# Two casts a head turned into transfers between SBUF rows in a fused attention and expert kernel

## The chip, the cores and the metric

The kernel runs on one core of a Trainium2 chip. The metric is the device time of one launch in microseconds (us). A core has five engines with queues of their own: TensorE (PE: matmuls, and transposes as matmuls with the identity), VectorE (DVE), ScalarE (ACT), GpSimd (POOL) and SyncE (SP), which here does nothing but issue DMA transfers. An engine takes its instructions in the order in which they were written; one that waits holds all behind it. Operands lie in SBUF (128 rows, called partitions), matmul results in PSUM.

## The reference

Three stages follow one another. Attention: 2 batches of 8 heads, 768 positions, 64 dimensions, where a query sees only keys of its own cluster. Then a layer of 8 experts of which each token uses one, and then a dense layer with softplus. The change lies in the first stage, whose core is

```python
mask = q_assign[:, :, :, None] == k_assign[:, :, None, :]
scores = scale * np.matmul(q, k.transpose(0, 1, 3, 2))
scores = np.where(mask, scores, -1000000000.0)
scores = scores - np.max(scores, axis=-1, keepdims=True)
attn = np.exp(scores)
attn = attn / (np.sum(attn, axis=-1, keepdims=True) + 1e-09)
return np.matmul(attn, v).astype(np.float32)
```

`q_assign` and `k_assign` are the indices of the nearest of 16 centroids.

## The kernel before

**Precision.** TensorE is fed with fp32r, a rounded form of fp32. To keep the accuracy of fp32, the kernel splits q and k into a rounded high part and the rest. A head has four operand tiles of 768 columns. Of the 128 rows of kA, 64 hold the high part of k and the other 64 the same high part again; of qA, 64 rows hold the high part of q / 8 and 64 its rest. A matmul of the two so gives (q high + q rest) times k high (L304). qB holds the high part of q in rows 0 to 63, kB the rest of k, and a second matmul adds their product (L319). Rows 64 to 79 of qB and kB hold the clusters of queries and keys as one-hot rows with large factors: where they differ, the score goes far down. So the mask is part of the second matmul. These 16 rows are called the cluster rows here.

**The loop.** The 16 heads have 6 query tiles each, which gives 96 blocks g = 6 h + t (L1092). Block g does, in this order: the products of attention weights and v of the head before (`av_step`), the scores of block g + 2 and their row maximum on VectorE (`S_mm`, L309, nm at L321), the six transposes of the weights of block g and the copies from PSUM to SBUF (`P_T`, L335), then jobs that a table puts into this block, the exponential of block g + 2 on ScalarE (`S_exp`, L330), the table `after`, and last a part of the preparation of a later head. Nothing reorders this: program order is queue order on each engine. Score tiles and transposes have two PSUM buffers each.

**Preparation.** Head h (2 to 15) is prepared in four parts, at the ends of blocks 6 (h - 2) + 3 to 6 (h - 2) + 6 (`prep_part`, L268): both halves of kA, kB, then qA and qB. Its first scores are written into block 6 h - 2. `put_mask` (L289) then issues four transfers of 16 x 384 words on SyncE's queue, which put the cluster rows of the head into qB and kB; for heads 3 to 15 this follows part 3.

**What else is in the queues.** Heads come in pairs p. `load_raw` (L168) loads q and k of a pair into one of two buffers; it is written into block 12 p - 25 and waits for the last reader of the buffer, qA of head 2 p - 3 on VectorE (L285). Sixteen further jobs convert a weight matrix from 64-bit words: `cv_load` (L435) brings 1 MB (words), `cv_bits` (L443) works on it in the four blocks from g0 = 11 + 19 j / 4 on, first on ScalarE (cvd, L451) and then on VectorE, and `cv_store` (L467) writes 512 KB back (w_rows). In the blocks g0 + 1 to g0 + 3 the set `busy` puts both PSUM copies of the transposes on ScalarE; in the others the first is on VectorE. `sims_mm` and `sims_T` assign the clusters of a later pair, `fin_x` (L379) transposes the outputs of an earlier head (L385).

Of the kernel before, what the change touches and what calls it, by code (L numbers as in the profile page):

```python
# [8 lines left out]
F32 = mybir.dt.float32  # L9
# [4 lines left out]
AF = mybir.ActivationFunctionType  # L14
# [18 lines left out]
def body(ctx, tc, qT, kT, vP, cen, mod, wg, bias, w1, w2, win, wout, out):  # L33
# [5 lines left out]
    NT = S // 128  # L39
# [7 lines left out]
    pe, dve, act, pool, sp = nc.tensor, nc.vector, nc.scalar, nc.gpsimd, nc.sync  # L47
# [102 lines left out]
    busy = set()  # L150
# [4 lines left out]
    def drain():  # L155
        while pend:
            for _ in pend.pop(0):
                pass

    def run(f, *a):  # L160

        drain()
        x = f(*a)
        if hasattr(x, "__next__"):
            next(x, None)
            pend.append(x)
# [101 lines left out]
    def prep_part(h, i):  # L268

        p, o = h // 2, 64 * (h % 2)  # L270
        if i == 0:
            spl[h] = tuple(p_sp.tile([128, S], F32R, tag=n, name=n) for n in ("qA", "kA", "qB", "kB"))
        qA, kA, qB, kB = spl[h]
        q_s, k_s = (r[o:o + 64] for r in raw[p])
        hi, lo = slice(o, o + 64), slice(64 - o, 128 - o)
        if i == 0:
            act.copy(kA[hi], k_s)
        elif i == 1:
            act.copy(kA[lo], k_s)
            dve.tensor_tensor(out=kB[0:64], in0=k_s, in1=kA[hi].bitcast(F32), op=ALU.subtract)  # L280
        elif i == 2:
            act.activation(out=qA[hi], in_=q_s, func=AF.Copy, scale=0.125)
        else:
            act.activation(out=qB[0:64], in_=q_s, func=AF.Copy, scale=0.125)
            dve.scalar_tensor_tensor(  # L285
                out=qA[lo], in0=q_s, scalar=0.125, in1=qA[hi].bitcast(F32), op0=ALU.mult, op1=ALU.subtract
            )

    def put_mask(h):  # L289
        p, i = h // 2, h % 2  # L290
        qA, kA, qB, kB = spl[h]
        for j, x in enumerate((qB, kB)):
            for a in range(2):
                o = 64 * j + 32 * a + 16 * i
                sp.dma_start(
                    out=x[64:80, a * HS:(a + 1) * HS].bitcast(F32), in_=mks[p][o:o + 16].bitcast(F32)
                )
# [11 lines left out]
    def S_mm(g):  # L309
        if g >= NH * NT:  # L310
            return
        if g not in S_t:
            S_part(g)
        h, t = divmod(g, NT)
        qA, kA, qB, kB = spl[h]
        ps = S_t[g]
        ts = slice(t * 128, t * 128 + 128)
        for i in range(2):
            pe.matmul(ps[:, i, :HS], qB[:80, ts], kB[:80, i * HS:(i + 1) * HS], start=False, stop=True)  # L319
        nm_t[g] = p_m.tile([128, 1], F32, tag="nm", name="nm", bufs=4)  # L320
        dve.tensor_reduce(out=nm_t[g], in_=ps[:, :, :HS], axis=AX.XY, op=ALU.max, negate=True)  # L321

    def S_exp(g):
        if g >= NH * NT:
            return
        h, t = divmod(g, NT)
        if t == 0:
            sums[h] = p_m.tile([128, NT], F32, tag="sums", name="sums", bufs=3)
        P_t[g] = p_P.tile([128, 2, HS], F32, tag="P", name="P")
        act.activation(  # L330
            out=P_t[g], in_=S_t.pop(g)[:, :, :HS], func=AF.Exp, bias=nm_t.pop(g), scale=1.0,
            accum_out=sums[h][:, t:t + 1],
        )

    def P_T(g):  # L335
        h, t = divmod(g, NT)
        if t == 0:
            PT[h] = p_PT.tile([128, NT, S], F32, tag="PT", name="PT")
        P = P_t.pop(g)
        for i in range(2):  # L340
            ps = ps_T.tile([128, 3, 128], F32, tag="t", name="Tp")
            for j in range(3):
                pe.transpose(ps[:, j, :], P[:, i, j * 128:(j + 1) * 128], ident)  # L343
            dst = PT[h][:, 3 * i:3 * i + 3, t * 128:(t + 1) * 128]
            if i == 0 and g not in busy:
                dve.tensor_copy(dst, ps)
            else:
                act.copy(dst, ps)  # L348
# [20 lines left out]
    def av_step(g):  # L369

        h, kt = divmod(g - NT - 1, NT)
        if kt == NT - 1:
            return
        AV(h, kt)
        if kt == NT - 2:
            AV(h, NT - 1)
            fin_av(h)
# [566 lines left out]
    with tc.manual_schedule():  # L944
# [147 lines left out]
        for g in range(NH * NT):  # L1092
            h, t = divmod(g, NT)
            if g > NT:
                av_step(g)
            S_mm(g + 2)
            P_T(g)
            for f, a in jobs.get(g, ()):
                if inspect.isgeneratorfunction(f):
                    run(f, *a)  # L1100
                else:
                    f(*a)
            S_exp(g + 2)
            drain()
            for f, a in after.get(g, ()):
                f(*a)
            h2, i2 = divmod(g - 3, NT)
            h2 += 2
            if 2 <= h2 < NH and i2 < 4:
                prep_part(h2, i2)  # L1110
                if i2 == 3 and h2 > 2:
                    put_mask(h2)
            if g == 8:
                put_mask(2)
# [299 lines left out]
        for n in range(2, end):  # L1414
            kind, i, layer, s = seq[n]
# [149 lines left out]
        for c, y in enumerate((ys[NM - 1][1], ps_A.tile([128, 512], F32, tag="a", name="o"))):  # L1565
            cs = slice(c * 256, c * 256 + 256)
            for kt in range(16):
                gh, gl = gs[NM - 1, kt // 4]
                hi, lo = wts["out", kt // 2]
# [51 lines left out]
```

## Time and profile before

| | |
|---|---|
| median of 3 runs (lowest, highest) | 767.64 us (766.39, 768.34) |
| the profiled execution: its time, its span | 767.36 us, 765.6 us |
| TensorE (PE) busy | 708.8 us, 93% of the span |
| VectorE (DVE) busy | 450.0 us, 59% |
| ScalarE (ACT) busy | 416.1 us, 54% |
| GpSimd (POOL) busy | 128.5 us, 17% |
| mean granted clock of TensorE | 0.975 |

The span runs from the first to the last instruction. Shares of it are means over stages that differ: in the attention part, the first 300 us, VectorE and ScalarE are busy to eight or nine tenths, later to two or three. A row of a timeline gives start and duration of an instruction, or of several alike that follow one another (x2), and in brackets how long the engine had stood idle before it and what ended that. The granted clock is that of TensorE as a share of 2.4 GHz.

### The profile page before, as it was taken

How to read it: one execution, taken by the hardware profiler on the slowest of the kernel's cores; microseconds unless marked ns; L12 is line 12 of the kernel's file. 1: busy time of each engine (PE TensorE's matmuls, PEld its weight loads, DVE VectorE, ACT ScalarE, POOL GpSimd, SP SyncE). 2: the span in 40 equal slices, each digit the busy share in tenths (PEclk: the TensorE clock that was granted, in tenths of full speed). 3: DMA queues.
4: the chain of work that ended last, by engine and by line, in shares of the span. 5: the costliest groups of instructions: out<-in, count | busy, mean ns of one | idle time of the engine just before them, and what ended most of it. 6: DMA issues, size and time to landing. Idle time of an engine off the chain costs nothing. (4 is left out here: it accounts for less than half of the span.)

```text
span 765.6 us, 11692 instructions
## 1 busy us (share of the span) xinstructions
PE 708.8 (93%) x4498; PEld 564.4 (74%) x4498; DVE 450.0 (59%) x668; ACT 416.1 (54%) x663; POOL 128.5 (17%) x144
## 2 busy tenths in 40 slices
PE   4997997899798999986999999998999999999998
PEld 2764654556455555874879888997998898999887
DVE  5895987789789975863446563677143233233220
ACT  3886987798779976343446562663323323323310
POOL 4200000000310103635452522252000000000000
PEclk9898999999989999996999999999999999999999
DMA  4314454544553625979967985500010000000000
GB/s 133 105 56 174 145 198 151 171 145 160 183 131 119 199 98 167 236 110 368 355 228 277 345 301 195 179 15 20 10 42 15 28 15 15 15 1 28 1 28 27
DMA packets 38683, 99.28 MB, mean 130 GB/s; under 512 B 8255, under 2 KB 15615, under 8 KB 36577
## 3 DMA queue, kind: packets, MB, share of 16 engines
q1 hardware_dynamic: 35888, 91.42, 36.3%
q0 software_dynamic: 2592, 6.69, 2.4%
q8 instruction: 36, 0.59, 0.3%
q10 hardware_dynamic: 144, 0.39, 0.2%
q14 instruction: 23, 0.18, 0.1%
HBM read 79.13 MB, written 18.28 MB: 127 GB/s over the span
## 5 line engine op out<-in xcount | busy, mean ns | idle before, releaser
L1500 DVE SCALAR_TENSOR_TENSOR sp<-g,sp 128x1024 f32<-128x1024 f32 x24 | 29.4, 1224 | 148.8 <-ACT sp L1499 148.8
L321 DVE TENSOR_REDUCE nm<-S 128x1 f32<-128x768 f32 x96 | 90.9, 948 | 34.3 <-PE S L319 34.0
L1489 PE MATMUL g<-xh,wh 128*128 128x256 f32 x384 | 108.7, 283 | 0.0
L1489 PE MATMUL g<-xh,wl 128*128 128x256 f32 x384 | 107.9, 281 | 0.0
L1489 PE MATMUL g<-xl,wh 128*128 128x256 f32 x384 | 107.9, 281 | 0.0
L1497 ACT ACTIVATE sp<-g 128x1024 f32<-128x1024 f32 x24 | 24.6, 1027 | 136.6 <-PE g L1489 126.7
L330 ACT ACTIVATE P<-S,nm 128x768 f32<-128x768 f32 x96 | 86.9, 905 | 18.9 <-DVE nm L321 16.2
L343 PE MATMUL Tp<-ident,P 128*128 128x128 f32 x576 | 85.6, 284 | 10.7 <-ACT PT L348 7.5
L343 PEld LDWEIGHTS Tp<-ident,P 128*128 128x128 f32 x576 | 68.7, 144 | 24.5 <-ACT PT L348 14.2
L355 PE MATMUL av<-PT,v 128*64 128x384 f32 x384 | 80.7, 517 | 0.0
L741 POOL TENSOR_TENSOR wl<-raw,wh 128x1024 fp32r<-128x1024 f32 x22 | 54.1, 2469 | 139.2 <-ACT wh L740 132.2
L741 DVE TENSOR_TENSOR wl<-raw,wh 128x1024 fp32r<-128x1024 f32 x50 | 65.1, 1343 | 14.5 <-ACT wh L740 14.5
L1489 PEld LDWEIGHTS g<-xl,wh 128*128 128x128 f32 x384 | 73.0, 190 | 0.5
L740 ACT CAST wh<-raw 128x1024 fp32r<-128x1024 f32 x69 | 68.9, 1050 | 8.0 <-DMA raw<-in_w 5.4
L1489 PEld LDWEIGHTS g<-xh,wh 128*128 128x128 f32 x384 | 72.8, 190 | 0.5
L348 ACT COPY PT<-Tp 128x384 f32<-128x384 f32 x144 | 64.0, 477 | 16.8 <-PE Tp L343 16.0
L1489 PEld LDWEIGHTS g<-xh,wl 128*128 128x128 f32 x384 | 73.0, 190 | 0.0
L1524 PE MATMUL o<-wh,gT 128*128 128x512 f32 x216 | 69.7, 394 | 0.0
L319 PE MATMUL S<-kB,qB 80*128 80x384 f32 x192 | 51.8, 353 | 18.0 <-DMA kB<-mk 16.1
L843 PE MATMUL y<-wh,hT 128*128 128x512 f32 x192 | 64.7, 408 | 0.0
L304 PEld LDWEIGHTS S<-kA,qA 128*128 128x128 f32 x192 | 29.7, 194 | 47.1 <-ACT PT L348 16.2
L304 PE MATMUL S<-kA,qA 128*128 128x384 f32 x192 | 60.2, 396 | 1.2 <-ACT P L330 0.9
(284 smaller groups left out, 1396.9 us busy)
## 6 DMA issues: line engine op xcount, KB each, us to landing
raw<-in_w SPq DMA_DIRECT2D x56, 512.0 KB, 7.6
words<-in_win SPq DMA_DIRECT2D x8, 1024.0 KB, 7.4
w_rows<-cvt SPq DMA_DIRECT2D x16, 512.0 KB, 3.0
words<-in_wout SPq DMA_DIRECT2D x8, 1024.0 KB, 5.7
whole<-in_w SPq DMA_DIRECT2D x16, 512.0 KB, 6.2
raw<-w_rows SPq DMA_DIRECT2D x16, 512.0 KB, 4.6
rawq<-in_qT SPq DMA_DIRECT2D x8, 384.0 KB, 3.4
v<-in_vP SPq DMA_DIRECT2D x8, 384.0 KB, 3.4
```

The source lines that it names most:

```text
L304: pe.matmul(ps[:, i, :HS], qA[:, t * 128:t * 128 + 128], kA[:, i * HS:(i + 1) * HS], start=True, stop=False)
L319: pe.matmul(ps[:, i, :HS], qB[:80, ts], kB[:80, i * HS:(i + 1) * HS], start=False, stop=True)
L321: dve.tensor_reduce(out=nm_t[g], in_=ps[:, :, :HS], axis=AX.XY, op=ALU.max, negate=True)
L330: act.activation(out=P_t[g], in_=S_t.pop(g)[:, :, :HS], func=AF.Exp, bias=nm_t.pop(g), scale=1.0, accum_out=sums[h][:, t:t + 1],)
L343: pe.transpose(ps[:, j, :], P[:, i, j * 128:(j + 1) * 128], ident)
L348: act.copy(dst, ps)
L355: pe.matmul(av_t[h][64 * a:64 * a + 64, :], vt[p][:, kt, 64 * i:64 * i + 64], PT[h][:, kt, a * HS:(a + 1) * HS], start=(kt == 0), stop=(kt ...
L740: cp(self.hi, self.raw)
L741: eng.tensor_tensor(out=self.lo, in0=self.raw, in1=self.hi.bitcast(F32), op=ALU.subtract)
L843: pe.matmul(u["y"][j], x, y, start=(kt == 0 and i == 0), stop=(kt == 7 and i == 2))
L1489: pe.matmul(o, a, b[:, kt, :], start=(n == 0 and f % 2 == 0), stop=(n == 11), skip_group_check=True)
L1524: pe.matmul(ys[u][j], x[:, a:a + 128], y, start=(kt == 0 and i == 0), stop=(kt == 15 and i == 2))
```

## The change

Per head the second casts are gone: the second half of kA (L279) and qB (L284) are no longer written by ScalarE but copied by a DMA from the rows that the first casts have written. The scaled cast of q moves from part 2 to part 1, the subtraction for kB on VectorE from part 1 to part 2. The cluster rows of heads 3 to 15 are issued after part 0 and no longer after part 3. In blocks with t = 0 and 1 that are not in `busy` the first PSUM copy goes to ScalarE too; the table gives 15 such blocks.

```diff
         if i == 0:
             act.copy(kA[hi], k_s)
+            sp.dma_start(out=kA[lo].bitcast(F32), in_=kA[hi].bitcast(F32))
         elif i == 1:
-            act.copy(kA[lo], k_s)
+            act.activation(out=qA[hi], in_=q_s, func=AF.Copy, scale=0.125)
+            sp.dma_start(out=qB[0:64].bitcast(F32), in_=qA[hi].bitcast(F32))
+        elif i == 2:
             dve.tensor_tensor(out=kB[0:64], in0=k_s, in1=kA[hi].bitcast(F32), op=ALU.subtract)
-        elif i == 2:
-            act.activation(out=qA[hi], in_=q_s, func=AF.Copy, scale=0.125)
         else:
-            act.activation(out=qB[0:64], in_=q_s, func=AF.Copy, scale=0.125)
             dve.scalar_tensor_tensor(
                 out=qA[lo], in0=q_s, scalar=0.125, in1=qA[hi].bitcast(F32), op0=ALU.mult, op1=ALU.subtract
             )
...
             dst = PT[h][:, 3 * i:3 * i + 3, t * 128:(t + 1) * 128]
-            if i == 0 and g not in busy:
+            if i == 0 and g not in busy and (g - 6) % NT not in (0, 1):
                 dve.tensor_copy(dst, ps)
...
                 prep_part(h2, i2)
-                if i2 == 3 and h2 > 2:
+                if i2 == 0 and h2 > 2:
                     put_mask(h2)
```

SyncE's queue before, from the loads of pair 3 on (blocks 11 to 16); qB<-mk and kB<-mk are the cluster rows, here of head 3, and the two words are those of the conversions j = 1 and 2:

```order
L173 DMA rawq<-in_qT 128x768
L174 DMA rawk<-in_kT 128x768
L438 DMA words<-in_win 128x2048
L295 DMA qB<-mk 16x384 x2
L295 DMA kB<-mk 16x384 x2
L469 DMA w_rows<-cvt 128x1024
L438 DMA words<-in_win 128x2048
```

The same place now, from the transfers of head 3 (block 9) on; the second kA<-kA and the cluster rows behind it are those of head 4:

```order
L278 DMA kA<-kA 64x768
L295 DMA qB<-mk 16x384 x2
L295 DMA kB<-mk 16x384 x2
L281 DMA qB<-qA 64x768
L173 DMA rawq<-in_qT 128x768
L174 DMA rawk<-in_kT 128x768
L438 DMA words<-in_win 128x2048
L469 DMA w_rows<-cvt 128x1024
L278 DMA kA<-kA 64x768
L295 DMA qB<-mk 16x384 x2
L295 DMA kB<-mk 16x384 x2
L438 DMA words<-in_win 128x2048
```

The cluster rows of head 3 moved from behind the loads and the first words to ahead of them, and the second words moved behind the transfer and the cluster rows of head 4.

ScalarE before, from the start of the conversion j = 1 (end of block 15) to block 17; PT<-Tp are the PSUM copies of the transposes, kA and qA those of head 4:

```order
L451 ACTIVATE cvd<-words 128x1024
L277 CAST kA<-rawk 64x768
L348 COPY PT<-Tp 128x3x128 x2
L330 ACTIVATE P,sums<-S,nm 128x768
L191 COPY sim<-misc 128x384
L279 CAST kA<-rawk 64x768
L362 COPY xTu<-av 128x384
L348 COPY PT<-Tp 128x3x128 x2
L330 ACTIVATE P,sums<-S,nm 128x768
L216 COPY simT<-misc 128x384
L282 ACTIVATE qA<-rawq 64x768
```

The same place now:

```order
L451 ACTIVATE cvd<-words 128x1024
L277 CAST kA<-rawk 64x768
L348 COPY PT<-Tp 128x3x128 x2
L330 ACTIVATE P,sums<-S,nm 128x768
L191 COPY sim<-misc 128x384
L280 ACTIVATE qA<-rawq 64x768
L362 COPY xTu<-av 128x384
L348 COPY PT<-Tp 128x3x128 x2
L330 ACTIVATE P,sums<-S,nm 128x768
L216 COPY simT<-misc 128x384
```

The cast of q took the place of the second cast of k in block 16, and nothing stands in its old place in block 17.

## Rows read from the trace of the kernel before

**Rows 1.** Waits of PE, 20 to 300 us: total us, times, longest us.

```profile
PE S L319 <- DMA kB<-mk: 16.1, 5, 5.1
PE Tp L343 <- ACT PT L348: 7.5, 12, 1.3
```

**Rows 2.** Timeline of PE: start us, us, engine, line, instruction, count [idle before].

```profile
63.09 0.98 PE L319 MATMUL S<-kB,qB 80*128 80x384 f32 x2 [4.35 <-DMA kB<-mk]
...
72.12 0.55 PE L385 MATMUL misc<-ident,xTu 128*128 128x128 f32 x3 [0.20 <-ACT simT L216]
...
97.64 0.58 PE L319 MATMUL S<-kB,qB 80*128 80x384 f32 x2 [1.09 <-DMA kB<-mk]
...
104.52 0.55 PE L385 MATMUL misc<-ident,xTu 128*128 128x128 f32 x3 [0.16 <-ACT simT L216]
...
136.06 0.98 PE L319 MATMUL S<-kB,qB 80*128 80x384 f32 x2 [5.11 <-DMA kB<-mk]
...
144.50 0.55 PE L385 MATMUL misc<-ident,xTu 128*128 128x128 f32 x3 [0.20 <-ACT simT L216]
...
207.95 1.01 PE L319 MATMUL S<-kB,qB 80*128 80x384 f32 x2 [4.25 <-DMA kB<-mk]
...
217.90 0.55 PE L385 MATMUL misc<-ident,xTu 128*128 128x128 f32 x3 [0.20 <-ACT simT L216]
```

**Rows 3.** Timeline of SyncE's DMA queue, 53 to 59 us.

```profile
53.40 0.34 SPq L173 DMA_DIRECT2D rawq<-in_qT  x1
...
54.25 0.43 SPq L438 DMA_DIRECT2D words<-in_win  x1
54.78 1.25 SPq L295 DMA_DIRECT2D qB<-mk  x2
...
58.85 0.43 SPq L438 DMA_DIRECT2D words<-in_win  x1
```

**Rows 4.** Timeline of ScalarE around the three long waits.

```profile
62.50 1.12 ACT L451 ACTIVATE cvd<-words 128x1024 f32<-128x1024 f32 x1 [3.33 <-DMA words<-in_win]
63.53 0.82 ACT L277 CAST kA<-rawk 64x768 fp32r<-64x768 f32 x1
...
69.95 0.86 ACT L348 COPY PT<-Tp 128x384 f32<-128x384 f32 x2 [0.74 <-PE Tp L343]
70.69 0.92 ACT L330 ACTIVATE P<-S,nm 128x768 f32<-128x768 f32 x1
...
71.58 0.49 ACT L216 COPY simT<-misc 128x384 f32<-128x384 f32 x1
71.94 0.85 ACT L282 ACTIVATE qA<-rawq 64x768 fp32r<-64x768 f32 x1
72.68 0.84 ACT L348 COPY PT<-Tp 128x384 f32<-128x384 f32 x2
...
79.15 1.14 ACT L451 ACTIVATE cvd<-words 128x1024 f32<-128x1024 f32 x1
...
135.41 1.12 ACT L451 ACTIVATE cvd<-words 128x1024 f32<-128x1024 f32 x1 [4.37 <-DMA words<-in_win]
...
207.37 1.12 ACT L451 ACTIVATE cvd<-words 128x1024 f32<-128x1024 f32 x1 [3.75 <-DMA words<-in_wout]
```

**Rows 5.** Busy time of each engine, granted clock (PEclk), DMA share, GB/s.

```profile
66.00:67.00 1.00, 1.00 (x10) 0.28 (x4) 1.00 (x2) 0.90 (x3) 0.00 (x0) 0.50 0.04 16
...
68.00:69.00 1.00, 1.00 (x8) 0.40 (x5) 0.00 (x0) 0.47 (x2) 0.00 (x0) 1.00 0.00 0
```

**Rows 6.** Groups by line and shape, whole span: busy us, mean ns.

```profile
L348 ACT COPY PT<-Tp 128x384 f32<-128x384 f32 x144 | 64.0, 477 | 16.8 <-PE Tp L343 16.0
...
L280 DVE TENSOR_TENSOR kB<-rawk,kA 64x768 fp32r<-64x768 f32 x14 | 13.3, 949 | 0.1
```

**Rows 7.** DMA issues at 126.5 and 101.8 us: count, KB, us to landing.

```profile
words<-in_win SPq DMA_DIRECT2D x1, 1024.0 KB, 8.9
...
words<-in_win SPq DMA_DIRECT2D x1, 1024.0 KB, 5.9
```

## The prediction, made before the changed kernel was run

> **What bounds the kernel now.** I read the page's slices first: TensorE is busy nearly everywhere, and most of its idle slices lie in the first 300 us, the attention part. The waits of TensorE between 20 and 300 us then say what it stood still for [rows 1]. One line leads: the matmuls on the cluster rows waited 16.1 us in 5 waits for the transfers that put those rows into kB. Waits for ScalarE's PSUM copies add 7.5 us in 12.
>
> The timeline of TensorE shows where the 5 are: at the first score tile of heads 3, 5, 7, 9 and 11. Four of them are in [rows 2]; at heads 3, 7 and 11 they are long (4.35, 5.11 and 4.25, together 13.7), at heads 5 and 9 short (1.09, and what is left of 16.1, 1.3). Each of these matmuls starts a sequence that ends with the transposes of L385. Undisturbed it takes 104.52 - 97.64 = 6.88 us. After the long waits it takes 72.12 - 63.09 = 9.03, 8.44 and 9.95, that is 2.15, 1.56 and 3.07 more, 6.8 in all. The clock explains most of this: from 66 to 67 us the granted clock is 0.50 (1.2 GHz) while TensorE is busy throughout, and 1.00 (2.4 GHz) again from 68 us [rows 5]; it stood still before the clock fell. So the waits and their aftermath cost 16.1 + 6.8 = 22.9 us.
>
> Why the rows came late is read from SyncE's queue [rows 3]. It issued the loads of the next pair at 53.40, a weight load of 1 MB at 54.25, and the cluster rows of head 3 only at 54.78, behind both.
>
> ScalarE's timeline [rows 4] shows what a quick reading misses. At the same three places ScalarE itself stood for 3.33, 4.37 and 3.75 us, until that 1 MB load (words) had landed, and resumed at 62.50, 135.41 and 207.37: 0.6 us before TensorE each time. Two waits lie side by side, and the change moves only one.
>
> **Part 1: the cluster rows go with the first cast.** They are now issued three blocks earlier (a block is one step of the attention loop), ahead of the pair's loads, on an otherwise free queue. A block lasts (97.64 - 63.09) / 12 = 2.9 us [rows 2], so they have seven blocks, 20 us, where 1 MB behind two loads needed 8.9 [rows 7]. All five waits for them go.
>
> At heads 5 and 9 nothing was beside it: 1.09 + 1.3 = 2.4 us gained.
>
> At heads 3, 7 and 11 the words are next late. TensorE can do the cluster matmuls and the next transposes, then needs PSUM copies that stand behind cvd on ScalarE. From the start of cvd, ScalarE has to do, up to the copy that lets L385 start: cvd (63.53 - 62.50 = 1.03), two 64-row casts (71.94 to 72.68, 0.74 each), two pairs of PSUM copies (69.95 to 70.69, 0.74 each), two exponentials (70.69 to 71.58, 0.89 each) and three single PSUM copies (71.58 to 71.94, 0.36 each): 1.03 + 1.48 + 1.48 + 1.78 + 1.08 = 6.85 us, start to start and without a gap [rows 4]. L385 then starts at 69.35, 142.26 and 214.22 where it was at 72.12, 144.50 and 217.90: 2.8 + 2.2 + 3.7 = 8.7 us, of 20.5 that a bare removal of the waits and the slow stretches would give there. The lower bound is nothing; the upper one is the 20.5.
>
> Do the words themselves land sooner? Before, a store and the next words (58.85) followed them closely. Now the next words stand behind the row transfer of head 4, which waits for ScalarE's cast after cvd, so they can't be in the way. With two loads ahead and such traffic behind, 1 MB landed in 8.9 us; with one load ahead in 5.9 [rows 7]. The difference of 3.0 bounds it, and zero is the other end; the loads ahead and the store stay, so I take 0.7 at each of three places, 2.1.
>
> That zero has a rule behind it. The Trainium skill (DMA: Bandwidth & Descriptors, Queues, rings and completion order) says that each DMA engine takes descriptors in ring order. By it what stands behind the words can't hold them, and the sum below would be 11.4 and the time 756.0; the two rows differ also in what stands ahead and do not decide it.
>
> **Part 2: casts become transfers.** 14 heads lose two casts each on ScalarE, 28 at 0.74, 20.7 us of busy time; 15 PSUM copies come to it (those not already there), at 0.477 [rows 6], 7.2 us. VectorE loses these 15. For TensorE this counts only where a PSUM copy was late behind a cast that goes. In the block where the second cast stood there is now another cast (qA), so most of the 7.5 us [rows 1] stay. I take 1.2. The ends are a gain of 7.5 and a loss of 7.2, should all moved copies be waited for.
>
> 28 transfers of 64 rows (192 KB) come to SyncE's queue. No row shows one. Their nearest rows are 1 MB in 5.9 and 8.9 us [rows 7], and they have six or seven blocks, 17 to 20 us, so they are hidden; what it costs when that cover goes is the fourth rival.
>
> **Part 3: kB one block later on VectorE.** In a stretch where VectorE has no gap, order costs nothing. Where it waits for TensorE just then, the subtraction (0.949 [rows 6]) delays qA, behind which the next pair's loads and then the words wait. At the three places this is between 0 and 2.8 us; I take one of three, 0.9 lost.
>
> **Sum.** 2.4 + 8.7 + 2.1 + 1.2 - 0.9 = 13.5 us. The work from 300 us on is unchanged and begins earlier, so I carry all of it. The profiled execution took 767.4 us (span 765.6 and 1.8 around it), 0.3 below the median of 767.6: 767.4 - 13.5 = 753.9, forecast 754.
>
> **Rivals.**
>
> *The words don't bind* (744). If ScalarE's lag is absorbed or the words come 3 us sooner, the waits and their slow stretches go whole: 22.9 + 1.2 = 24.1, 743.3. For it: the words had up to 3.0 us of disturbed landing. Against: at 62.50 ScalarE itself was released only 0.6 us before TensorE.
>
> *The clock falls all the same* (761). In the forecast TensorE still has short gaps at each of the three places, in the first for copies behind cvd. If the clock goes to 1.2 GHz as in [rows 5], the 6.8 us stay: 767.4 - 6.7 = 760.7. For it: ScalarE still stands at the words. Against: after the 1.09 us wait at head 5 the sequence ran its 6.88 us at full pace.
>
> *The words alone set these places* (765). Then only the short waits go: 767.4 - 2.4 = 765.0, hardly more than can be told from no change. Against it: after 63.53 ScalarE waited for TensorE again ([rows 4] has 0.74 us at 69.95).
>
> *The next words come too late* (773, slower). Behind head 4's row transfer the second words are issued not at 58.85 but after ScalarE's cast (63.53 + 0.82), the transfer and four cluster rows (two take 1.25 [rows 3]): about 67.4. ScalarE wants them at 79.15 [rows 4], by the forecast 2.8 earlier, 76.4. Up to 9.0 us of landing are hidden: both of 5.9 and 8.9 fit, the second by 0.1. Each us beyond is a wait of ScalarE, and long ones cost the slow stretch too, 2.3 a place. It happens at three places (heads 4, 8, 12) and outweighs the 13.5 from a landing of about 11.2 us on (3 x (2.2 + 2.3) = 13.5). At 13 us it costs 3 x (4.0 + 2.3) = 18.9, net 5.4 slower, 772.8.
>
> **How the numbers follow.** Forecast 0.55, words don't bind 0.13, clock falls 0.20, words alone 0.07, too late 0.05. 0.3% is 2.3 us, about the least that measurements of this kernel tell from none. Forecast, first and second rival are faster by more: 0.88. Words alone sits on the edge: same, 0.07. Slower 0.05. The range from 744 to 763 takes in the second rival and the first down to its end; outside are the last two and the tail of the first, 0.18.
>
> **What would show it.** No TensorE wait on kB's cluster rows at heads 3 to 11; ScalarE still waiting for words at cvd three times, 2 to 4 us each; L385 about 6.9 us behind each of these; granted clock 1.00 after them; 28 fewer casts and 15 more PSUM copies on ScalarE; no wait on kA or qB rows. I am wrong if ScalarE's waits for words vanish (first rival), if half speed stays behind them (second), or if new waits for words stand at heads 4, 8 and 12 (fourth).

## The result and the profile after

The changed kernel took 758.32 us (median of 4 runs, 754.63 to 759.47) beside 767.1 for the kernel before on the same chip: a ratio of 0.987, interval 0.982 to 0.991. The profiled execution took 759.41 us (span 757.7) where that of before took 767.36: 7.95 us less, at a mean granted clock of 0.986. The forecast was 754, a gain of 13.5; the gain is real, and about 5 us smaller (8.8 by the medians). What follows is read from the one profiled execution. The lowest of the four, 754.63, lies at the forecast; what differed in it no profile shows.

Waits of TensorE between 20 and 300 us (total us, times, longest us), the answer to [rows 1]:

```profile
PE Tp L343 <- ACT PT L348: 9.6, 11, 1.6
PE S L319 <- DMA qB<-qA: 4.9, 1, 4.9
```

The 16.1 us in which the matmuls waited for the cluster rows are gone. In their place stands one wait of 4.9 us for a transfer that did not exist before: the copy of q's high part from qA into qB.

TensorE's timeline after (start us, us, engine, line, instruction, count, idle before), the answer to [rows 2]: L385 behind the preparation of heads 3, 7 and 11, then head 12:

```profile
65.64 0.92 PE L343 MATMUL Tp<-ident,P 128*128 128x128 f32 x6 [1.62 <-ACT PT L348]
...
70.37 0.55 PE L385 MATMUL misc<-ident,xTu 128*128 128x128 f32 x3 [0.71 <-ACT simT L216]
...
137.45 0.51 PE L385 MATMUL misc<-ident,xTu 128*128 128x128 f32 x3
...
205.00 0.81 PE L385 MATMUL misc<-ident,xTu 128*128 128x128 f32 x3
...
219.18 0.92 PE L319 MATMUL S<-kB,qB 80*128 80x384 f32 x2 [4.95 <-DMA qB<-qA]
...
226.23 0.49 PE L385 MATMUL misc<-ident,xTu 128*128 128x128 f32 x3
```

Against [rows 2] L385 comes 72.12 - 70.37 = 1.75 us earlier at head 3, 144.50 - 137.45 = 7.05 at head 7 and 217.90 - 205.00 = 12.90 at head 11. Up to there the forecast is nearly met. Then head 12 gives back: its L385 stands 21.23 us behind that of head 11, where it was 15.87 in the kernel before (it began at 233.77). The lead is 7.54 after that, and what the execution keeps is 7.95.

ScalarE's timeline after, at cvd, the first work on each MB of words (the answer to [rows 4]):

```profile
63.38 1.12 ACT L451 ACTIVATE cvd<-words 128x1024 f32<-128x1024 f32 x1 [2.71 <-DMA words<-in_win]
76.96 1.14 ACT L451 ACTIVATE cvd<-words 128x1024 f32<-128x1024 f32 x1
...
130.41 1.12 ACT L451 ACTIVATE cvd<-words 128x1024 f32<-128x1024 f32 x1 [3.08 <-DMA words<-in_win]
...
197.98 1.14 ACT L451 ACTIVATE cvd<-words 128x1024 f32<-128x1024 f32 x1 [3.04 <-issue]
216.64 1.12 ACT L451 ACTIVATE cvd<-words 128x1024 f32<-128x1024 f32 x1 [4.40 <-DMA words<-in_wout]
```

ScalarE still stands for the words at the same three places, 2.7 to 3.1 us each. (The third row names no releaser; run 5 below, in which these words come earlier, has no wait there.) L385 starts 70.37 - 63.38 = 6.99, 7.04 and 7.02 us after cvd; the prediction had added up 6.85, with the last copy (simT) at 0.36 from start to start, where L385 waits for its end, 0.48 to 0.49. At 76.96 (head 4) the next words are in time. The last row is new: at head 12 the words were late too.

Busy time of each engine after, PEclk, DMA share, GB/s; the two stretches of [rows 5] at head 3:

```profile
66.00:67.00 1.00, 0.56 (x5) 0.31 (x3) 0.97 (x3) 1.00 (x3) 0.00 (x0) 1.00 0.66 138
...
68.00:69.00 1.00, 0.77 (x5) 0.46 (x5) 1.00 (x2) 1.00 (x4) 0.00 (x0) 1.00 0.13 32
```

and the same stretch behind the cvds of head 7 (130.41) and head 11 (197.98):

```profile
134.00:136.00 2.00, 1.70 (x7) 1.70 (x8) 2.00 (x3) 2.00 (x6) 0.00 (x0) 0.50 0.34 72
...
202.00:204.00 2.00, 2.00 (x9) 1.87 (x10) 2.00 (x4) 2.00 (x5) 1.78 (x2) 0.54 0.31 52
```

At head 3 the clock stays at 2.4 GHz (1.00). At heads 7 and 11 it did go to 1.2 GHz (0.50) for about 3 us. ScalarE is busy for the whole of both stretches (2.00 of 2.00). simT, the copy that L385 waits for, at heads 3, 7 and 11:

```profile
69.83 0.49 ACT L216 COPY simT<-misc 128x384 f32<-128x384 f32 x1
...
136.87 0.48 ACT L216 COPY simT<-misc 128x384 f32<-128x384 f32 x1
...
204.46 0.48 ACT L216 COPY simT<-misc 128x384 f32<-128x384 f32 x1
```

It ends 0.05, 0.10 and 0.06 us before L385, which follows cvd by the same 7.0 us at either clock. At half speed TensorE has used up the gap of 0.71 us that it had at head 3, and arrives no later. So in this stretch ScalarE sets the end, and TensorE's clock costs next to nothing.

The jam of head 12, first in SyncE's queue, with the words loads of the four late cvds:

```profile
55.02 0.42 SPq L438 DMA_DIRECT2D words<-in_win  x1
...
122.28 0.42 SPq L438 DMA_DIRECT2D words<-in_win  x1
...
189.74 0.42 SPq L438 DMA_DIRECT2D words<-in_wout  x1
...
202.95 0.58 SPq L438 DMA_DIRECT2D words<-in_wout  x1
203.63 0.50 SPq L281 DMA_DIRECT2D qB<-qA  x1
```

GpSimd at the same time: the first and the last of six scatters that write the token list of the expert stage (`scatter_list`; 128 single words each, issued at L589):

```profile
195.18 1.20 POOL L589 DMA_INDIRECT token_list<-tokid,ridx  x1 [17.80 <-DVE cnt L529]
...
202.26 1.77 POOL L589 DMA_INDIRECT token_list<-tokid,ridx  x1 [0.22 <-issue]
```

Busy time, clock, DMA share and GB/s in the same stretch:

```profile
200.00:205.00 5.00, 4.03 (x19) 3.33 (x20) 4.93 (x10) 5.00 (x13) 3.59 (x5) 0.72 0.56 69
205.00:210.00 5.00, 5.00 (x29) 3.32 (x29) 4.24 (x7) 2.84 (x7) 0.00 (x0) 0.94 0.92 44
```

DMA issues from 202.9 to 204 us (count, KB, us to landing):

```profile
words<-in_wout SPq DMA_DIRECT2D x1, 1024.0 KB, 13.7
qB<-qA SPq DMA_DIRECT2D x1, 192.0 KB
...
token_list<-tokid,ridx POOLq DMA_INDIRECT x1, 16.6
```

From 205 to 210 us the DMA engines are 0.92 busy and move 44 GB/s. The words needed 13.7 us, against 5.9 at best in [rows 7], and qB, issued behind them at 203.63 and without a landing in the trace, released TensorE only at 219.18. Elsewhere these row transfers are short; those of L281 whose landing the trace shows, in us:

```profile
DMA to landing us min/median/max: 2.6/2.7/2.9
```

### The profile page after: what moved, and what is told of

Read it like the earlier page. It is cut to its first block, busy times and chain, and to the rows that moved or that the text cites. A ratio compares the mean times of both kernels' runs of the same rounds, so it can differ in the third digit from the quotient of the medians.

```text
span 757.7 us, 11736 instructions
## 1 busy us (share of the span) xinstructions
PE 704.7 (93%) x4498; PEld 566.5 (75%) x4498; DVE 443.8 (59%) x653; ACT 396.9 (52%) x650; POOL 128.1 (17%) x144
## 5 line engine op out<-in xcount | busy, mean ns | idle before, releaser
L343 PEld LDWEIGHTS Tp<-ident,P 128*128 128x128 f32 x576 | 69.8, 145 | 22.9 <-ACT PT L348 14.7
L348 ACT COPY PT<-Tp 128x384 f32<-128x384 f32 x159 | 70.2, 484 | 14.6 <-PE Tp L343 13.9
## 6 DMA issues: line engine op xcount, KB each, us to landing
words<-in_wout SPq DMA_DIRECT2D x8, 1024.0 KB, 13.7
```

## The experiments

Times are medians in us, beside the kernel before on the same chip. "Early rows" is the cluster rows at part 0, "late" at part 3; "early words" loads j = 1, 6 and 11 one block earlier.

| kernel | time | before | ratio (interval) |
|---|---|---|---|
| changed kernel | 758.32 | 767.1 | 0.987 (0.982 to 0.991) |
| 1 before + early rows | 758.69 | 768.42 | 0.988 (0.985 to 0.992) |
| 2 changed, late rows | 773.39 | 768.42 | 1.006 (1.003 to 1.009) |
| 3 changed, casts in head 12 | 755.99 | 768.42 | 0.983 (0.981 to 0.986) |
| 4 changed, scatters at block 70 | 752.49 | 768.42 | 0.980 (0.978 to 0.983) |
| 5 changed + early words | 762.52 | 770.2 | 0.990 (0.987 to 0.993) |
| 6 before + early words | 759.81 | 770.2 | 0.986 (0.983 to 0.990) |
| 7 as 5, scatters at block 70 | 752.44 | 770.2 | 0.975 (0.971 to 0.979) |
| 8 changed, no moved copies | 759.92 | 769.24 | 0.989 (0.986 to 0.991) |
| 9 as 1, next words later | 767.05 | 770.2 | 0.996 (0.994 to 0.999) |
| 10 as 5, scatters in two groups | 751.05 | 769.24 | 0.975 (0.973 to 0.978) |
| 11 as 10, casts kept | 745.0 | 769.24 | 0.969 (0.967 to 0.971) |
| 12 before, scatters at block 70 | 771.52 | 769.24 | 1.004 (1.002 to 1.006) |

**Which part did it? Runs 1 and 2.** Run 1 makes the one move alone, run 2 all but it.

```diff
-                if i2 == 3 and h2 > 2:
+                if i2 == 0 and h2 > 2:
```

> One part alone: only the cluster rows are issued three blocks earlier; the four casts a head and the PSUM copies stay as before. Theory A (the early rows give the gain; the transfers that replace casts give little up to head 11 and cost about 5 us at head 12, where one of them, qB, lands late): about 755, with waits for words at cvd as after, the start of L385 of head 9 (193.8 before, 184.8 after) near 185 to 187, and no wait on a qB transfer at head 12. Rival B (the casts that left ScalarE give a good part of the gain): 760 or more.

> The rest of the change without the early rows: casts become transfers and PSUM copies move, but the cluster rows follow part 3 as before. Theory A: the five waits on the cluster rows are back (about 16 us of TensorE), so 765 to 770. Rival B (gain from ScalarE's relief): 758 to 761.

Run 1 gains what the whole change gains, but took 758.69 where about 755 was expected, and its L385 of head 9 is at 188.33, not at 185 to 187. Run 2 is slower than the kernel before, and than the 765 to 770 expected. Its waits of TensorE, the five of before again:

```profile
PE S L319 <- DMA qB<-mk: 9.0, 2, 4.8
PE S L319 <- DMA kB<-mk: 7.9, 3, 5.0
```

The early rows carry the gain. Run 1 and the changed kernel reach it by different ways, as L385 at heads 11 and 12 in run 1 shows:

```profile
210.08 0.55 PE L385 MATMUL misc<-ident,xTu 128*128 128x128 f32 x3 [0.64 <-ACT simT L216]
225.59 0.49 PE L385 MATMUL misc<-ident,xTu 128*128 128x128 f32 x3
```

At head 11 the changed kernel is 210.08 - 205.00 = 5.1 us ahead of run 1, at head 12 0.6 behind (226.23). So the rest of the change is worth 5 us up to there and loses it at one place.

**What is the wait at head 12? Runs 3 and 4.** Run 3 keeps four casts in head 12 alone; run 4 moves the six scatters six blocks back.

```diff
-            sp.dma_start(out=kA[lo].bitcast(F32), in_=kA[hi].bitcast(F32))
+            if h != 12:
+                sp.dma_start(out=kA[lo].bitcast(F32), in_=kA[hi].bitcast(F32))
...
```

```diff
-        job(64, r0_scatter)
+        job(70, r0_scatter)
```

> The changed kernel, with head 12 alone prepared by four casts as before (its second casts in the blocks of the first two casts of k and of part 2, no row transfers). Theory A (the row transfer of qB of head 12 stands behind 1 MB of words that six scatters of single words hold up): the 4.95 us wait at head 12 is gone, words of that place are issued earlier and ScalarE's 4.4 us wait there shrinks; 753 to 755, and a smaller spread from run to run than after (754.6 to 759.5). Rival C (the late qB only hides a wait for the words, which stays): about 757.

> The changed kernel with the six scatters of the token list six blocks later (block 70 in place of 64), away from the transfers of head 12. Theory A: no wait on qB at head 12 and no ScalarE wait for the words there, 753 to 755; the words of a later block may be late instead for 1 to 3 us. Rival C: the wait at head 12 comes from its place behind 1 MB of words alone and stays: 758.

Both remove the wait. By the ratios run 3 is 0.4% below the changed kernel, 2.7 us, which the intervals don't part, and its spread of 4.5 us is hardly smaller (4.8 there). Head 12 does lose nothing in it (L385 at 207.88 for head 11 and 223.56 for head 12, 15.68 apart), but at head 11 it is 2.9 us behind the changed kernel: without the row transfers of head 12 the next words are issued 5.80 us behind those of head 11, not 13.21, and cvd starts 9.84 us after their issue, not 8.24. Run 4 is 0.7% below, 5.1 us, about what head 12 had lost, and its interval and the changed kernel's only touch. qB stands behind 1 MB of words there as well (201.76 behind 201.08), so that place alone does not make the wait. The slow stretch of the DMA engines moved with the scatters, which run from 211.31 to 219.83 there; busy time, clock, DMA share and GB/s in run 4:

```profile
205.00:210.00 5.00, 5.00 (x32) 3.36 (x31) 4.90 (x10) 3.19 (x8) 0.00 (x0) 1.00 1.04 325
...
220.00:225.00 5.00, 4.37 (x29) 2.93 (x29) 4.84 (x10) 3.77 (x8) 0.00 (x0) 1.00 0.91 85
```

Run 12 is the control: the later scatters alone, on the kernel before.

> The kernel before with the six scatters at block 70 in place of 64 and nothing else. Theory A (before, the slowed transfers hit nothing urgent, the changed kernel put urgent ones there): no change, 766 to 770. Rival F (the place of the scatters is a gain of its own): 761 to 764.

It is slightly slower (771.52, expected 766 to 770), with one more wait for cluster rows, so the scatters' place has no worth of its own; it matters through what runs beside them.

**Two waits side by side? Runs 5 and 6.** The words of the three places are loaded one block earlier, in the changed kernel and in the kernel before.

```diff
-            job(g0 - 4, cv_load, j)
+            job(g0 - 4 - (j in (1, 6, 11)), cv_load, j)
```

> The changed kernel, with the 1 MB words of the conversions 1, 6 and 11 issued one block earlier, ahead of the loads of the next pair. Theory A (after the early rows these words are what is late at heads 3, 7 and 11): ScalarE's waits of 2.7, 3.1 and 3.0 us at cvd are gone and L385 follows the first score matmul of heads 3, 7 and 11 within about 7 us; the wait at head 12 stays; 750 to 753. Rival D (ScalarE and VectorE are the bound there anyway): 757 to 759.

> The kernel before, with the same three words one block earlier and nothing else. Theory A (two waits lie side by side at heads 3, 7 and 11; the cluster rows were late because 1 MB stood ahead of them): the cluster rows then stand behind two loads alone, as at heads 5 and 9, TensorE's waits for them shrink from 4 to 5 us to about 1, the clock stays at full speed, ScalarE doesn't wait at cvd; 750 to 755. Rival E (the rows were late because SyncE waits for qA on VectorE, whatever stands between): waits as before, 765 to 768.

Both totals missed, run 5 by more than 9 us. Yet up to head 11 the mechanism holds: no cvd waits for words any more, and L385 there is at 196.66 in run 5 and 198.62 in run 6, that is 21.2 and 19.3 us ahead of [rows 2]. Head 12 then took it back. TensorE in run 5:

```profile
196.66 0.55 PE L385 MATMUL misc<-ident,xTu 128*128 128x128 f32 x3 [0.34 <-ACT simT L216]
...
219.49 0.98 PE L319 MATMUL S<-kB,qB 80*128 80x384 f32 x2 [12.64 <-DMA qB<-qA]
```

and in run 6:

```profile
198.62 0.55 PE L385 MATMUL misc<-ident,xTu 128*128 128x128 f32 x3 [0.64 <-ACT simT L216]
...
216.64 1.01 PE L319 MATMUL S<-kB,qB 80*128 80x384 f32 x2 [9.01 <-DMA kB<-mk]
```

Run 6 has no row transfers. Its cluster rows, issued at 201.46 right behind scatters that ran from 191.66 to 200.2, landed some 15 us later:

```profile
201.46 1.21 SPq L295 DMA_DIRECT2D kB<-mk  x2
```

So the jam comes with the scatters and hits whatever is urgent then; the row transfers of the changed kernel are one such victim. In the profiles of the changed kernel, run 6 and run 5 the wait is the longer, the earlier L385 of head 11 starts: 4.95 us after 205.00, 9.01 after 198.62, 12.64 after 196.66.

**Both causes away. Runs 7, 10 and 11.** Run 7 is run 5 with the scatters at block 70. Runs 10 and 11 issue them one in every second block from 66 on; run 11 keeps the kernel before's casts and copies, so it has no row transfers.

```diff
-            scatter_list(0, tmp["idx"])
+            for t in range(NT):
+                job(66 + 2 * t, scatter_one, t)
...
```

> The changed kernel with both: the three words one block earlier and the scatters at block 70. Theory A: no wait for words at the three places and none at head 12; the gains add: 745 to 748.

> The changed kernel, the three words one block earlier, and the six scatters of the token list not in a row but one in every second block from 66 to 76. Theory A (six scatters in a row slow the large transfers that are under way; the lead of about 21 us that early rows and early words give up to head 11 is lost there only in part): no TensorE wait on qB of head 12 and no long one later, 747 to 751. Rival G (any scatter beside large transfers costs the same): 753 or more.

> As the run with early words and spread scatters, but with the four casts a head and the PSUM copies as before: early rows, early words, spread scatters. Theory A (casts turned into transfers are worth 1 to 3 us where nothing jams): 749 to 753, and 1 to 3 us above that run. Rival B (ScalarE's relief is worth more): 755 or more.

Run 7 fell short: the jam moved to head 13, where qB was 2.94 us late. In runs 10 and 11 GpSimd did not issue evenly, but two scatters near 190 and four from 204 to 210, and run 10 kept a wait for qB at head 12 where none was expected. TensorE in run 10:

```profile
195.87 0.55 PE L385 MATMUL misc<-ident,xTu 128*128 128x128 f32 x3 [0.36 <-ACT simT L216]
208.05 0.73 PE L319 MATMUL S<-kB,qB 80*128 80x384 f32 x2 [2.74 <-DMA qB<-qA]
215.11 0.49 PE L385 MATMUL misc<-ident,xTu 128*128 128x128 f32 x3
...
233.82 0.49 PE L385 MATMUL misc<-ident,xTu 128*128 128x128 f32 x3
```

and in run 11:

```profile
195.85 0.55 PE L385 MATMUL misc<-ident,xTu 128*128 128x128 f32 x3 [0.64 <-ACT simT L216]
211.36 0.49 PE L385 MATMUL misc<-ident,xTu 128*128 128x128 f32 x3
228.36 0.49 PE L385 MATMUL misc<-ident,xTu 128*128 128x128 f32 x3
```

The two are level at head 11, then the one with the casts is 3.75 and 5.46 us ahead. Run 11, at 745.0, is the best of all; its profile shows no wait of TensorE for a DMA in the attention part after 20 us. I had expected it 1 to 3 us behind run 10; the sign was wrong. Without late words the casts turned into transfers gain nothing that shows up to head 11, and cost 6 us in total (751.05 to 745.0; that is the casts, the copies and kB's place together), nearly all of it at heads 12 and 13.

**The smaller terms. Runs 8 and 9.** Run 8 drops the moved PSUM copies (the condition `(g - 6) % NT not in (0, 1)`). Run 9 is run 1 with the words that follow the three places two blocks later (`g0 - 4 + 2 * (j in (2, 7, 12))`).

> The changed kernel without the moved PSUM copies: in blocks with t = 0 and 1 the first copy stays on VectorE. Theory A: the copies are worth at most 1.5 us either way; 757 to 760. Rival H (VectorE's relief carries the gain before head 11): 761 or more.

> The early rows alone (casts as before), with the words of conversions 2, 7 and 12 issued two blocks later, so that they no longer follow the words of 1, 6 and 11 by 6 us. If what follows on the queue slows a transfer that stands ahead: from issue to the start of cvd the words of 6 and 11 take about 8.2 us, as in the changed kernel, and not 9.8 and 9.4 as with the early rows alone, and the time is 755 to 757. If a transfer is served in order (the ring rule): 9.4 to 9.8 stay and the time is about 758.5.

Run 8 equals the changed kernel within the intervals (by the ratios it is 1.3 us above): the copies are worth nothing that can be told from none. Its DMA engines are slow at the same place, 0.97 busy at 48 GB/s from 205 to 210 us, but TensorE waits only 0.15 us for qB at head 12, and L385 there is 17.88 us behind head 11's. So the same jam can cost less; with one profile each, whether by the execution or by the edit stays open. Run 9 missed. The three loads took 7.13, 9.11 and 10.02 us from issue to cvd, in run 1 8.19, 9.84 and 9.38: 1.1 us less in sum. The delayed words themselves were then late at head 12, in run 9:

```profile
223.19 1.12 ACT L451 ACTIVATE cvd<-words 128x1024 f32<-128x1024 f32 x1 [6.46 <-DMA words<-in_wout]
```

## Why the prediction was right in its direction and too high in its gain

**The five waits.** They are gone, as said, and at heads 5 and 9 the lead grew by 1.53 and 1.77 us from one L385 to the next, 3.3 where 2.4 was forecast.

**The words as the next wait.** Shown. The cvd waits stayed, L385 follows cvd by 7.0 us, and at heads 3, 7 and 11 the lead grew by 2.18, 3.63 and 3.92 (the first from a start that was 0.43 behind), 9.7 where 8.7 + 2.1 - 0.9 = 9.9 was forecast. Runs 5 and 6 confirm the pair of waits from the other side: with the words early too, heads 3 to 11 gain 19 to 21 us, near the 20.5 given for a bare removal of the waits and 22.9 with all five. The rivals "the words don't bind" and "the words alone" fall with this.

**The clock.** "Granted clock 1.00 after them" was wrong at two of three places: the event of the second rival happened at heads 7 and 11. Its price did not follow. I had charged it the 6.8 us of the slow stretches of before, but the lead grew there as the forecast had it, since ScalarE's chain, 6.85 us by the forecast and 7.0 measured, just covers TensorE at half speed. The forecast was right here with a reason that was partly wrong.

**The words landing sooner (2.1).** Too large against the kernel before: issue to cvd was 8.25, 8.93 and 8.45 us, and is 8.36, 8.13 and 8.24, 0.9 less in sum. Run 9 took the next words further away from run 1's and won 1.1. Both sums are small, and single loads went either way, up by 0.6 in run 9. Against the kernel before alone this is nearer to the rule in the Trainium skill (DMA: Bandwidth & Descriptors, Queues, rings and completion order), that descriptors are taken in ring order, than to my term. The runs with early rows lean towards my term. Where the next words were issued some 13 us behind (changed kernel, runs 4 and 8, heads 3 and 7 of run 3), 11 loads took 7.52 to 8.76 us, 8.1 in the mean; where they were issued 6 to 8 us behind (runs 1 and 9, head 11 of run 3), 7 loads took 7.13 to 10.02, 9.1 in the mean, about 0.9 more, where my term had 0.7 a place. The two groups differ in casts and row transfers too, so what holds the words is open.

**kB one block later (0.9 lost).** No run moves it alone; what it cost is not shown.

**Casts and copies (1.2).** Run 8 can't tell the copies from nothing. Against run 1 everything but the early rows is worth 5.1 us up to head 11, and 4.8 of it is there when cvd starts (197.98, in run 1 202.81): there the words are issued 3.7 us earlier and land 1.1 faster. How much of this the casts gave by themselves, no run shows. Where no words are late, runs 10 and 11 give nothing up to head 11.

**The step that failed** is "they have six or seven blocks, 17 to 20 us, so they are hidden". For the other row transfers it holds as far as the trace shows their landing, 2.6 to 2.9 us for qB and up to 4.7 for kA against 17, and TensorE waits for none of them. At head 12 it is false: the transfer stood behind 1 MB of words while the scatters were under way, landed after more than 15 us, and took 5.4 of the 12.9 us that had been won, with a slow stretch behind it (granted clock 0.56 from 219 to 221 us). The fourth rival had the queue (words pushed behind a row transfer, too late at head 12), with a chance of 0.05 and three places; its like came true at one place, because of a burst on another queue that neither the forecast nor the rival looked at. The sign was in the trace of before: the words issued at 203.38 there landed after 14.0 us beside the same scatters, needed only at 225.60. I had read landing times at two other places alone. These 5.4 us are nearly all of the 13.5 - 7.95 = 5.6 that were missing.

**Open.** Why the six scatters slow large transfers: run 10 shows 39 GB/s at a DMA share of 0.76 between 196 and 200 us, with no scatter being issued then. No run took the scatters out altogether.

## What to carry to other kernels

When a wait is to be removed, look at every engine that resumes within a microsecond of it: the next wait is already there and sets what is gained. Before an instruction is turned into a transfer, find the slowest landing in that part of the program and what else the DMA engines do then; here a cast of 0.74 us in order on an engine was better than a transfer of 2.7 us that once took 15. And a gain early in a program moves later work onto other bursts, so the lead has to be followed, place by place, to the end.

## What was unexpected of the hardware

Six scatters of 128 single words, a few KB in all, went with a DMA share of 0.92 at 44 GB/s, 1 MB landing in 13.7 us where 5.9 was seen elsewhere, and cluster rows of 24 KB in some 15 us (run 6) where transfers of the kind landed in 1.9 to 2.3 between 60 and 120 us of the changed kernel. In run 6 the rows came 16 us after the last scatter's issue; in the changed kernel a scatter itself landed after 16.6 us.

The granted clock stayed at 1.00 at head 3, behind gaps of 1.62, 0.70, 0.23 and 0.71 us, and fell to 0.50 at heads 7 and 11, behind gaps of 1.27 and 0.70, and 1.10 and 0.70. What tells these apart no run shows. The slow stretches at these two heads came without a wait of 4 to 5 us like those that stood ahead of them in the kernel before.
